# A sigmoid attention and token-mixing MLP kernel: a new hand-written order of its steps, loads, casts and PSUM banks

## Chip, core and metric

The kernel runs on one core of one Trainium2 chip. The metric is the device time of one execution in microseconds (us). The core has TensorE (PE in the profile; PEld are its weight loads), VectorE (DVE), ScalarE (ACT), GpSimd (POOL), and SyncE (SP), which issues most DMAs.

## The reference

Eight batches, twelve heads, 448 positions, head size 64. First attention with a sigmoid in place of a softmax, then a token-mixing MLP on its output:

```python
def _attn_ref(q, k, v):                       # q, k, v: 8 x 12 x 448 x 64, float32
    scores = scale * np.matmul(q, k.transpose(0, 1, 3, 2)) - np.log(S)
    attn = 1.0 / (1.0 + np.exp(-scores))
    return np.matmul(attn, v)

def _moe_ref(x, w_q, w_k, w_out):             # x: 8 x 448 x 768
    wq = x @ w_q                              # w_q, w_k: 768 x 64
    wk = x @ w_k
    W_tok = scale * np.einsum('bsd,btd->bst', wq, wk)
    mixed = np.einsum('bst,btd->bsd', W_tok, x)
    return np.maximum(mixed, 0.0) @ w_out     # w_out: 768 x 768
```

## The kernel before

**Tiling.** Heads are taken in groups of four, called quads; a batch has three, so there are 24, numbered 0 to 23. The positions of a quad are cut into 7 pieces of 64. For each piece `scores` (L319) runs four matmuls of 64 x 64 x 448 on the four quadrants of the PE array into a pair of PSUM banks, and ACT takes the sigmoid of the pair into one of 16 `at` buffers (L324): 168 such steps. `values` (L341) multiplies `at` by v and gathers the 7 pieces of a quad in another pair of banks; an eviction (L348, L350) puts the result into `xt`, transposed, and `tr_x` turns it to `xn` on PE with one eviction (L363 with 128 x 128 matmuls, or L379 with four times as many small ones; L368, L392).

**MLP.** When the three quads of a batch are there, `mlp_wqk` makes wq and wk (L416 with whole matmuls, L404 tiled into quadrants; the tiled form adds two halves with one more eviction, L411, L412), `mlp_wkn` transposes wk (L431, L437), `mlp_tmp` multiplies it by x (L445 whole, L460 tiled; L449, L464, L465), and `mlp_mix` makes the mixed rows (L484, L498), with scale and ReLU in the eviction (L469 on ACT, L471 on DVE). Pairs of batches then go through w_out in output blocks: `out_pair` (L530, evicted by L541 or L543) for batches 2 to 5, `out_halves` (L571; L576, L577) and `out_chunk` (L612; L645, L634) for the rest. Results go to one of three `o` buffers and from there to DRAM by DMAs that SP issues (L552, L585, L622), a few at the end by ACT.

**q and k.** They are loaded in float32 (L173, L179), into one of eight `ld` buffers that v's loads share, and cast to bfloat16 on POOL or DVE (L192, L215; v's casts are L209). Then their transposes: for most quads POOL swaps 32-partition blocks (L161, L164, L167) and DVE transposes 32 x 32 blocks (L276); for seven quads DVE does all (L269, L245); for a few PE transposes (L229, L237) and DVE evicts (L293, L307). The cast tiles of q and k have two buffers, those of v four.

**The order.** Nothing is scheduled at run time or by the compiler: each engine runs its instructions in the order in which the program issues them, and four tables set that order. `PLAN` is a string with a letter for each step: S a score piece, P (R, p) a piece of values, q, c, e, r and their partners the transposes, x and X the turn to `xn`, W (L, l, w) a step of wq and wk, N, U and T, M, O (Q, o, I, i) the MLP's steps, 1 a cast by DVE; variants of a letter choose the engine of an eviction or the tiled form. `BANKS` names the banks each step takes, in the same order. `ORDER` lists loads and casts; a dot ahead of an item says that DVE casts it when PLAN has a 1, all others are cast by POOL as soon as `ready` allows (buffers, and the cast of the quad before). `pump_loads` issues loads through SP in the order of `ORDER`, as long as the load eight places before has been cast in program order. From the load number `LATE` on it also stops after two loads until an output block is finished:

```python
            late = len(ring) > LATE
            if late and not allowed[0]:
                break
```

A load on SP waits for the cast that frees its buffer; what stands behind it on SP waits as well.

Of the kernel before, what the change touches and what calls it, by code (L numbers as in the profile page):

```python
# [17 lines left out]
def kernel(  # L18
# [29 lines left out]
    def pool(name, bufs, **kw):  # L48
# [16 lines left out]
    banks16 = banks.rearrange("p b x -> p (b x)").bitcast(BF16).rearrange("p (b x) -> p b x", b=8)  # L65

    BANKS = (
# [11 lines left out]
    )  # L79
    BANKS = BANKS.split()[::-1]  # L80

# [43 lines left out]
    def xt(u, j):  # L125
# [4 lines left out]


    PLAN = (
        "FFSSSFFKSSF1S1abSSSSSPrPsPSPSzPqSkSSP1PSPSxPSrPSSPSPsPPPPPPP"
        "SPPSSzWWWSWWWSxSSrXSNPsPPPPSPSPUSzSPPPSRMSPPPSqkSSXMSSMSRPPC"
        "SP1xSPPPcSSWWWxSWdWSWSQSrNsSSOOOSPPPSPPSPzPISISISISPPPPPSPSc"
        "PodoSSxUSPPMSPRPSPPScWQWSdMSWWoWWSMPPSPPrPSPPSNQosSSzSQOQxSO"
        "SXSSQcOdSCTSRPCrSPPPSCPPPPPSPPSPPCSOsWQSzSSWWoOSxWWWSPPMSPPP"
        "PRCSSScXXoodXSMNSQocSMPPSPPPSPPSUSdQSMQSoMocdSPPPPPPSPSWWXWS"
        "MSWWWXSSoNOSTSOcSOSrOQSQdSOSPPPPGRPSPsSPPRPPSPPSzoQSOSXSORPP"
        "SPScPPPoS1oSxQSOSLLLSdLLRLPSPPPPSPSoomcoQSNoGdSQxSQQST11PRSP"  # L140
        "RSPPRSooQcGOdcSSQOSQSOoSOSMoQGPPRSRPxPSPdQSQSOcSxQLLLSpLLSLP"
        "PpSPPPdSoSoxSo1SOSQOSOSNOStpRSRPSPPPRpSPpRypyplloGlGlllMQQyN"
        "QiTiiimIIGIMioOQOOQOQOQOQQoooOOOQ"
    )
    KIND = ["a"] + [t for t in PLAN if t in "qacer"]

# [546 lines left out]
    for t in wqks:  # L693
# [1 line left out]


    ORDER = (
# [4 lines left out]
    )  # L702
    BY = {"s": [], "v": []}
    for x in ORDER.split():
# [7 lines left out]
    done = dict.fromkeys("SPqkKxWNUMOCgz", 0)  # L712
    used, loaded, cast = set(), set(), set()

    LATE = 33
    ring = [("q", 0), ("k", 0)]

    allowed = [2]
# [1 line left out]
    def pump_loads():  # L720
        while len(loaded) < len(ORDER):

            late = len(ring) > LATE
            if late and not allowed[0]:
# [196 lines left out]
```

## Time and profile before

| | us |
|---|---|
| median of 3 runs (lowest, highest) | 183.65 (183.09, 185.05) |
| the profiled execution, its own time | 182.08 |
| its span in the profile | 180.3 |
| busy: PE, ACT, DVE, POOL | 168.8, 161.0, 144.7, 117.4 |
| HBM read, written | 35.78 MB, 11.01 MB |

The profile is of one execution. Busy time of PE is modelled: matmuls are pipelined and four quadrant matmuls run at once, so the mean time of one (357 ns for L319) is longer than the spacing of their starts. Times in the stretches below count from the start of the span. The granted TensorE clock is at 0.9 or more of full speed in all 40 slices of the page.

### The profile page before, as it was taken

How to read it: one execution, taken by the hardware profiler on the slowest of the kernel's cores; microseconds unless marked ns; L12 is line 12 of the kernel's file. 1: busy time of each engine (PE TensorE's matmuls, PEld its weight loads, DVE VectorE, ACT ScalarE, POOL GpSimd, SP SyncE). 2: the span in 40 equal slices, each digit the busy share in tenths (PEclk: the TensorE clock that was granted, in tenths of full speed). 3: DMA queues.
4: the chain of work that ended last, by engine and by line, in shares of the span. 5: the costliest groups of instructions: out<-in, count | busy, mean ns of one | idle time of the engine just before them, and what ended most of it. 6: DMA issues, size and time to landing. Idle time of an engine off the chain costs nothing.

```text
span 180.3 us, 7877 instructions
## 1 busy us (share of the span) xinstructions
PE 168.8 (94%) x3431; PEld 116.1 (64%) x3431; DVE 144.7 (80%) x230; ACT 161.0 (89%) x213; POOL 117.4 (65%) x160
## 2 busy tenths in 40 slices
PE   7867799989999999999999999999999999999990
PEld 7433456454476465656667788788888878787560
DVE  3667899999998899989989799987897976678401
ACT  4699999999999999999999999999999999966250
POOL 1074798992899999999999999999879410010000
PEclk9999999999999999999999999999999999999999
DMA  5999999998998899999999929779997432405686
GB/s 168 345 396 385 329 382 397 398 233 181 349 386 296 312 284 346 305 319 275 266 407 323 335 81 276 284 209 315 278 333 204 114 91 62 120 4 126 165 242 175
DMA packets 24787, 47.31 MB, mean 262 GB/s; under 512 B 3760, under 2 KB 18352, under 8 KB 24752
## 3 DMA queue, kind: packets, MB, share of 16 engines
q1 hardware_dynamic: 23472, 44.64, 76.3%
q0 software_dynamic: 800, 1.18, 3.6%
q10 hardware_dynamic: 480, 0.98, 1.7%
q8 instruction: 27, 0.44, 1.0%
q14 instruction: 8, 0.07, 0.1%
HBM read 35.78 MB, written 11.01 MB: 260 GB/s over the span
## 4 chain that ended last, share of the span: by engine, by line
PE 78%; DVE 13%; ACT 5%; issue 1%
PE banks L319 16%; PE banks L530 15%; PE banks L341 13%; PE banks L612 13%; ACT at L324 5%; PE banks L571 3%; PE banks L416 3%; DVE xt L350 3%; DVE qk L245 3%; PE banks L363 2%; PE banks L379 2%; PE banks L690 2%; PE banks L404 2%; PE banks L460 2%; DVE mx L471 2%; PE banks L484 1%
## 5 line engine op out<-in xcount | busy, mean ns | idle before, releaser
L324 ACT ACTIVATE at<-banks 128x896 bf16<-128x896 f32 x168 | 140.3, 940 | 2.0 <-PE banks L319 1.3
L319 PE MATMUL banks<-qk 64*64 64x448 bf16 x672 | 62.5, 357 | 5.1 <-ACT at L324 2.5
L341 PE MATMUL banks<-at,v 64*64 64x448 bf16 x672 | 45.7, 350 | 0.4 <-ACT at L324 0.4
L319 PEld LDWEIGHTS <-qk 64*64 64x64 bf16 x672 | 26.4, 105 | 24.2 <-issue 14.9
L530 PE MATMUL banks<-wout,mx 64*64 64x384 bf16 x672 | 36.1, 323 | 0.0
L192 POOL CAST qk<-k 128x896 bf16<-128x896 f32 x19 | 22.8, 1202 | 10.1 <-DMA k<-in_k_dram 9.7
L341 PEld LDWEIGHTS <-v 64*64 64x64 bf16 x672 | 23.7, 106 | 6.9 <-POOL v L209 0.8
L530 PEld LDWEIGHTS <-mx 64*64 64x64 bf16 x672 | 23.9, 107 | 3.5 <-issue 0.5
L192 POOL CAST qk<-q 128x896 bf16<-128x896 f32 x18 | 21.6, 1197 | 4.4 <-DVE qk L276 4.0
L350 DVE CAST xt<-banks 128x896 bf16<-128x896 f32 x21 | 22.6, 1081 | 2.2 <-PE banks L341 2.0
L612 PE MATMUL banks<-wout,mx 128*128 128x384 bf16 (+1 forms) x138 | 24.1, 320 | 0.0
L471 DVE TENSOR_SCALAR mx<-banks 128x1024 bf16<-128x1024 f32 (+3 forms) x23 | 21.2, 933 | 2.9 <-PE banks L484 1.9
L209 POOL CAST v<-v 128x896 bf16<-128x896 f32 x21 | 19.4, 933 | 1.6 <-DMA v<-in_v_dram 1.3
L612 PEld LDWEIGHTS <-mx 128*128 128x128 bf16 x138 | 12.5, 98 | 9.6 <-issue 2.5
L245 DVE STREAM_TRANSPOSE qk<-qk 32x448 f32<-32x448 f32 x28 | 17.8, 636 | 0.8
L161 POOL COPY swap<-qk 32x448 uint32<-32x448 uint32 x26 | 14.7, 565 | 2.8 <-DVE qk L192 1.3
L276 DVE STREAM_TRANSPOSE qk<-qk 128x448 f32<-128x448 f32 x26 | 16.1, 629 | 0.1
L164 POOL COPY qk<-qk 32x448 uint32<-32x448 uint32 x26 | 14.4, 554 | 1.5
L167 POOL COPY qk<-swap 32x448 uint32<-32x448 uint32 x26 | 14.4, 552 | 1.5
L413 POOL COPY wq<-wqk 64x448 bf16<-64x448 bf16 x3 | 1.7, 554 | 17.7 <-DVE wqk L412 17.7
L645 ACT COPY o<-banks 128x384 f32<-128x384 f32 x13 | 6.3, 483 | 5.7 <-PE banks L612 4.9
L392 DVE COPY xn<-banks 128x1024 bf16<-128x1024 bf16 (+1 forms) x15 | 9.5, 632 | 1.6 <-PE banks L379 1.4
(88 smaller groups left out, 203.3 us busy)
## 6 DMA issues: line engine op xcount, KB each, us to landing
q<-in_q_dram SPq DMA_DIRECT2D x24, 448.0 KB, 6.8
v<-in_v_dram SPq DMA_DIRECT2D x24, 448.0 KB, 6.7
k<-in_k_dram SPq DMA_DIRECT2D x23, 448.0 KB, 6.3
out_dram<-o SPq DMA_DIRECT2D x50, 192.0 KB, 4.1
wout<-in_moe_w_out_dram POOLq DMA_DIRECT2D x2, 576.0 KB, 9.1
wout<-wout SPq DMA_DIRECT2D x4, 288.0 KB, 9.8
out_dram<-o ACTq DMA_DIRECT2D x4, 192.0 KB, 3.5
k<-in_k_dram SPq DMA_DIRECT2D x1, 256.0 KB, 4.5
```

The source lines that it names most:

```text
L161: eng.tensor_copy(out=z[lo], in_=w[hi, 0])
L192: COPY[e](out=f[:, :, "qk".index(nm)].rearrange("p e i d y -> p e y i d"), in_=ld.pop((nm, n)).rearrange("p (y i e d) -> p e y i d", y=2, ...
L209: COPY[e](out=t16.rearrange("p b i d -> p (b i d)"), in_=ld.pop((nm, n)).rearrange("p b x -> p (b x)"),)
L245: nc.vector.transpose(out=qk[n][other : other + 32, h].rearrange("p t i n -> p (t i n)").bitcast(F32), in_=w[own : own + 32, 1 - h],)
L276: nc.vector.transpose(out=qk[n][:, t].rearrange("p t i n -> p (t i n)").bitcast(F32), in_=w)
L319: nc.tensor.matmul(sc[HALF[h], g, 0:S], qk[n][HALF[g], h, 1, i, :], qk[n][HALF[g], h, 0].rearrange("p i n -> p (i n)"), start=True, stop=True,
L324: inst = nc.scalar.activation(at, sc[:, :, 0:S], ACTF.Sigmoid, bias=attn_bias, scale=attn_scale)
L341: nc.tensor.matmul(ps[HALF[g], h, 0:S], ld["v16", n][HALF[h], g, i, :], ats[n, i][HALF[h], g, :], start=(i == 0), stop=(i == NI - 1),)
L350: read(fb, COPY[eng](out=xt(u, j)[:, :, 0:S], in_=ps[:, :, 0:S]))
L471: inst = nc.vector.tensor_scalar(dst, ps, moe_scale, 0.0, ALU.mult, ALU.max)
L530: nc.tensor.matmul(ps[HALF[x], y, 0:NB], mx[HALF[y], u, b, 64 * (i - 3 * y) : 64 * (i - 3 * y) + 64], wout16[HALF[y], b // 2, swapped(y, b ...
L612: nc.tensor.matmul(ps, mxs[w][:, 2 * S * c + m * P : 2 * S * c + (m + 1) * P], wout16[:, c, 0, w0:w1], start=(c == 0), stop=(c == NC - 1),)
```

## The change

`PLAN`, `BANKS`, `ORDER` and `LATE` are replaced; the code that reads them is not. The number of casts that DVE makes at a 1 in PLAN goes from eight (q1, k1, q4, k8, v19, v20, q22, v23) to nine (q1, k1, k2, q2, v8, q13, v15, v22, v23). The limit `LATE` goes from 33 to 69 of 73 loads. In PLAN the numbers of most letters stay; two batches' `mlp_tmp` change from the tiled to the whole form (T to U), one batch's `mlp_wqk` from tiled to whole with the second copy on ACT (L to w), two quads' `tr_x` from small to whole transposes (x to X), and some evictions change between DVE and ACT. PE has 3353 matmuls in place of 3431. The first and last lines of each table and the two small edits:

```diff
     BANKS = (
-        "01 23 45 7 7 67 01 23 5 5 45 67 01 4 45 23 67 01 23 45 67 01 23 45 67 23 45 23 67 45 23 "
+        "01 23 45 7 7 67 01 23 5 5 45 67 01 4 45 23 67 01 67 45 23 01 67 45 23 01 45 23 67 45 23 "
...
     PLAN = (
-        "FFSSSFFKSSF1S1abSSSSSPrPsPSPSzPqSkSSP1PSPSxPSrPSSPSPsPPPPPPP"
+        "FFSSSFFKSSF11SSab1SSSSSRSP1SPrPPsRzPRPSPPSPPqSPkSXSxSrSPPSR"
...
-        "QiTiiimIIGIMioOQOOQOQOQOQQoooOOOQ"
+        "ONIiItiiiimiGMOoQOoQoOQoQOoOoQQooo"
...
     ORDER = (
-        ".q1 .k1 k2 q2 v0 q3 k3 .q4 v1 k4 v2 w0 q5 k5 v3 q6 v4 k6 .k8 k7 w1 v5 w4 q7 q8 q9 v6 k9 "
+        ".q1 .k1 .k2 .q2 v0 v1 q3 k3 k4 q4 v2 w0 v3 k5 q5 q6 v4 k6 w1 k7 w4 v5 q7 q8 k8 q9 v6 k9 "
...
-    LATE = 33
+    LATE = 69
```

Two places where instructions move. The first is on DVE at the start, from the casts of quad 1 on. A number behind a name tells tiles apart: before, qk_260 holds the cast q and k of quad 2 and qk_357 those of quad 4; xt_111 to xt_113 are the first three quads' attention outputs. Before:

```order
L215 CAST q_247<-q_181 128x2x7x64
L215 CAST k_256<-k_183 128x2x7x64
L293 COPY qk<-banks 128x7x2x64 x2
L269 STREAM_TRANSPOSE qk<-qk_260 128x448 x2
L245 STREAM_TRANSPOSE qk<-qk_260 32x448 x4
L307 COPY qk<-banks 128x2x2x448
L192 CAST qk_357<-q_195 128x2x2x224
L350 CAST xt_111<-banks 128x2x448
L392 COPY xn<-banks 128x2x4x128
L269 STREAM_TRANSPOSE qk<-qk_357 128x448 x2
```

On the same engine and from the same place now; qk_286 holds quad 2 and qk_372 quad 4:

```order
L215 CAST q_251<-q_181 128x2x7x64
L215 CAST k_255<-k_183 128x2x7x64
L293 COPY qk<-banks 128x7x2x64 x2
L192 CAST qk_286<-k_185 128x2x2x224
L192 CAST qk_286<-q_187 128x2x2x224
L269 STREAM_TRANSPOSE qk<-qk_286 128x448 x2
L245 STREAM_TRANSPOSE qk<-qk_286 32x448 x4
L350 CAST xt_111<-banks 128x2x448
L350 CAST xt_112<-banks 128x2x448
L307 COPY qk<-banks 128x2x2x448
L368 COPY xn<-banks 128x4x256
L392 COPY xn<-banks 128x2x4x128
```

Both casts of quad 2 have come from POOL to DVE, ahead of quad 2's transposes; the cast of q4 has gone to POOL; and two evictions to xt stand ahead of L307, quad 3's last step, where one stood behind it.

The second place is on SP, where the first output blocks of `out_pair` are stored (L552). Loads are L173 and L179; the number is that of the `ld` tile. Before:

```order
L179 DMA v_2124<-in_v_dram 128x2x448
L173 DMA q_2126<-in_q_dram 128x896
L552 DMA out_dram<-o 64x2x384 x2
L179 DMA v_2294<-in_v_dram 128x2x448
L173 DMA k_2296<-in_k_dram 128x896
L552 DMA out_dram<-o 64x2x384 x2
L173 DMA k_2504<-in_k_dram 128x896
L173 DMA q_2506<-in_q_dram 128x896
L552 DMA out_dram<-o 64x2x384 x2
```

And now, from the same first store on:

```order
L552 DMA out_dram<-o 64x2x384 x2
L173 DMA k_2352<-in_k_dram 128x896
L179 DMA v_2354<-in_v_dram 128x2x448
L173 DMA q_2358<-in_q_dram 128x896
L173 DMA k_2362<-in_k_dram 128x896
L179 DMA v_2365<-in_v_dram 128x2x448
L173 DMA k_2369<-in_k_dram 128x896
L179 DMA v_2452<-in_v_dram 128x2x448
L173 DMA k_2456<-in_k_dram 128x896
L173 DMA q_2466<-in_q_dram 128x896
L552 DMA out_dram<-o 64x2x384 x4
```

Two loads stood between two blocks' stores; now nine do, and two blocks' stores follow each other behind them.

More of the change, by code (lines that the diff above doesn't have):

```diff
@@ L132 @@
     PLAN = (
-        "FFSSSFFKSSF1S1abSSSSSPrPsPSPSzPqSkSSP1PSPSxPSrPSSPSPsPPPPPPP"
[L134 to L142, printed above, removed]
-        "QiTiiimIIGIMioOQOOQOQOQOQQoooOOOQ"
+        "FFSSSFFKSSF11SSab1SSSSSRSP1SPrPPsRzPRPSPPSPPqSPSkSXSxSrSPPSR"
+        "sSPPPPSWWWSSWWzWxSNSrSUPPSPPSPPsPSPPPSPPCzSMSPPSSMqSkSXCSMPS"
+        "PRPSRxSPPSQScxSdWrWSSWWWWSsSOOSNOSRPPSPPPzPSiSISIcISPPSPdPPP"
+        "SPSQQS1xSUSPPMScPPPPSPSWdWQWSSMWWWoMCSPRSPRrPRSSPOQCNSsSSQzO"
+        "OSxOSXCcSSQOdSTSRP1PSPPRSPRPSPPPrSPSPooCsWWSSSWzWWWOQxSPRSPc"
+        "MPSRPRNXSSSdXXoOSMSOOSMPPSPPPScPPSUQSdSMQQSQPcSPRPGPPPSSXd1W"
+        "WSSWWWWXSQSNQcSdGOOSQSorSUSQSOpSRRRSRPsSPRpPSPPPPSQSOSQSRzpO"
+        "cSPRRPSPOSQSQdGQSSwXXwwwwwXSRNRoGpcSOSpdPpPSQSOS1oOSMQSoUcdS"
+        "pRSoRPSpPPSoSoGOSocSQSQOSoSQSxQGQGSPPpRpRSpo1OdSQSOLLSLLLcSL"
+        "PRPSPPpdSPOSoxSOxOSQSQSONQPSxRSPPpPSPtRPSpllPypPRlMlOmlMloxo"
+        "ONIiItiiiimiGMOoQOoQoOQoQOoOoQQooo"
     )
```

26 rows, old and new, of tables (BANKS, ORDER) are left out of this document.

## The prediction, made before the changed kernel had run

> **What bounds the kernel now.** First the page's busy times, then the span cut into stretches (columns: stretch, its length, and for PE, PEld, DVE, ACT and POOL the busy time with the number of instructions; then granted clock, DMA share, GB/s).
>
> ```profile
> PE 168.8 (94%) x3431; PEld 116.1 (64%) x3431; DVE 144.7 (80%) x230; ACT 161.0 (89%) x213; POOL 117.4 (65%) x160
> ...
> 20.00:60.00 40.00, 37.62 (x766) 21.77 (x766) 37.41 (x55) 39.73 (x50) 32.65 (x44) 1.00 1.00 328
> 60.00:101.60 41.60, 41.59 (x694) 25.64 (x687) 39.08 (x57) 41.05 (x53) 39.36 (x53) 1.00 0.98 318
> 101.60:155.60 54.00, 54.00 (x1378) 44.44 (x1374) 44.09 (x67) 52.93 (x70) 37.23 (x52) 1.00 0.68 207
> 155.60:176.20 20.60, 20.51 (x396) 14.72 (x388) 11.75 (x25) 11.54 (x24) 0.55 (x1) 1.00 0.52 133
> 176.20:180.30 4.10, 0.00 (x0) 0.00 (x0) 0.31 (x1) 0.00 (x0) 0.00 (x0) 0.95 0.56 169
> ```
>
> ACT is full to 155.6 us, PE reads as full from 60 us, and POOL and DVE lack 2.2 and 2.5 us of being full from 60 to 101.6. The cut at 101.6 is the 112th score (of 168): the score line alone has 444 matmuls in the window ahead of it, and 4 ran before 6.7 us, so 448, or 112 scores of 4.
>
> ```profile
> 6.70:101.60 94.90, 39.88 (x444) 16.64 (x436) 1.00 1.00 330
> ```
>
> Next the ACT rows: the timeline's first, then the ACT groups of 6.7 to 101.6 us (count, then busy time and mean), then those of 101.6 to 156.45 us.
>
> ```profile
> 6.74 18.82 ACT L324 ACTIVATE at<-banks 128x896 bf16<-128x896 f32 x23 [0.69 <-PE banks L319]
> ...
> L324 ACT ACTIVATE at<-banks 128x896 bf16<-128x896 f32 x110 | 91.1, 949 | 1.2 <-PE banks L319 0.9
> L645 ACT COPY o<-banks 128x384 f32<-128x384 f32 x6 | 2.9, 487 | 0.0
> L543 ACT COPY o<-banks 128x768 f32<-128x768 f32 x1 | 0.8, 800 | 0.2 <-PE banks L530 0.2
> L348 ACT CAST xt<-banks 128x448 bf16<-128x448 f32 x1 | 0.5, 532 | 0.1
> ...
> L469 ACT ACTIVATE mx<-banks 128x512 bf16<-128x512 f32 (+1 forms) x5 | 3.4, 689 | 0.1
> L541 ACT COPY o<-banks 128x384 f32<-128x384 f32 x4 | 2.0, 494 | 0.2 <-ACT at L324 0.2
> ```
>
> Unhindered sigmoids start every (18.82 - 0.94) / 22 = 0.81 us, so one overlaps the next by 0.13. From 6.7 to 101.6: 110 x 0.81 = 89.4, eight other ACT instructions 4.2, less their overlap of about 1.0; of 94.9 us some 2 are stalls. This stretch is bound by ACT.
>
> Last the PE groups from 101.6 to 176.2 us, whose busy times overlap, and from the chain of waits the time that a block takes when PE is not held up (start, time, count).
>
> ```profile
> L530 PE MATMUL banks<-wout,mx 64*64 64x384 bf16 x624 | 33.4, 323 | 0.0
> L319 PE MATMUL banks<-qk 64*64 64x448 bf16 x232 | 22.5, 351 | 0.0
> L341 PE MATMUL banks<-at,v 64*64 64x448 bf16 x252 | 17.3, 350 | 0.0
> L612 PE MATMUL banks<-wout,mx 128*128 128x384 bf16 (+1 forms) x66 | 10.0, 311 | 0.0
> L404 PE MATMUL banks<-xt,wqk 64*64 64x448 bf16 x72 | 5.1, 349 | 0.0
> L379 PE MATMUL banks<-ident,xt 64*64 64x64 bf16 x256 | 3.6, 193 | 0.0
> L460 PE MATMUL banks<-xn,wkn 64*64 64x384 bf16 x56 | 3.3, 323 | 0.0
> ```
>
> ```profile
> 50.74 0.38 PE banks L341 x8
> 63.62 0.38 PE banks L416 x2
> 69.90 0.38 PE banks L379 x32
> 87.81 0.45 PE banks L363 x8
> 92.60 0.77 PE banks L445 x8
> 95.38 0.49 PE banks L530 x12
> 128.58 0.59 PE banks L460 x14
> 166.20 9.93 PE banks L612 x66
> ```
>
> L530 costs 0.0408 us a matmul: 624 make 25.5, and the 96 of L571, same shape, 3.9. At 0.0475 (L341's 0.38 / 8) the 232, 252 and 72 of L319, L341 and L404 make 26.4. L612 adds 9.9, L379 3.0, L460 2.4: 71.1. Another 112 small matmuls cost at most 5.3 by L341's price. So of 74.6 us no more than 3.5 can be idle: from the 112th score PE's own work sets the time, and the last 4.1 us are the final eviction and store. The program's time is ACT's way to the 112th score, plus PE's work from there, plus 4.1.
>
> **The change part by part.** The sum is made on the profiled run, 182.08 us: the span of 180.3 and 1.78 around it. The median of the runs shown, 183.65, is 1.57 above that; I add the sum to the median.
>
> *PE's work after the 112th score.* By the two programs: 12 fewer L530 (-0.49), 24 fewer L404 (-1.14), 28 fewer L460 (-1.18), 64 fewer L379 (-0.76); 16 more L445 (+1.54), 6 more L416 (+1.14), 16 more L363 (+0.90), 8 more of 256 columns (at most +0.38). Sum +0.4, on the path. Bounds: 0, if the small prices are high, and +1.1, if ACT makes PE wait in the first 14 of the 56 scores (there the work is 11.3 us at these prices, below the 11.4 of 14 sigmoids and one more ACT instruction beside them, which makes 12.0). I take +0.4.
>
> *ACT to the 112th score.* Now five L645 copies, one half L348, one L541, one half L469, against six L645, one L543, one L348: five of 0.487 + 0.532 + 0.494 + 0.60 = 4.06, against 4.25. So -0.2. After it the others grow from 6.4 us (3.4 and 2.0, and two single ones of half a tile, about 0.5 each like L348's) to about 7.8: six halves of L469 at 0.60 (four halves are the 3.4 less about 1.0 for the whole one), three L541, one L543, and three single ones, a whole xt of about 0.95 (a sigmoid's size) and two halves. With 56 x 0.81 = 45.5 and less overlap of 1.5 that makes 51.8, under PE's 54.0: hidden. If the 2.2 us of cover went, it would cost up to 1.4.
>
> *The start: two casts come from POOL to DVE.* The rows that price it:
>
> ```profile
> 10.09 1.15 DVE L293 COPY qk<-banks 128x896 bf16<-128x896 bf16 x2 [0.70 <-PE banks L237]
> 11.06 1.19 POOL L192 CAST qk<-q 128x896 bf16<-128x896 f32 x1
> 13.49 2.64 DVE L245 STREAM_TRANSPOSE qk<-qk 32x448 f32<-32x448 f32 x4
> 17.43 0.38 PE L319 MATMUL banks<-qk 64*64 64x448 bf16 x4 [0.21 <-ACT at L324]
> 40.89 1.37 DVE L192 CAST qk<-k 128x896 bf16<-128x896 f32 x1
> 117.74 0.67 DVE L209 CAST v<-v 128x896 bf16<-128x896 f32 x1
> ```
>
> POOL's cast of q2 ends at 12.25 and the transposes of quad 2 end at 16.13 (13.49 + 2.64), so they take 3.88. The first score of quad 2 starts at 17.43, held by ACT: 1.3 us of slack. Now DVE casts both behind its copies, from 11.24, at 0.67 (the quickest such row) to 1.37 (the slowest): done 12.6 to 14.0, transposes 16.5 to 17.9. Against 17.43 that is 0.9 early to 0.5 late; +0.1. POOL is free of two casts there, which is worth nothing: it waits for loads.
>
> *The other casts.* Before, k8 (1.37) and q4 were DVE's in 20:60; now they are POOL's, and v8 comes instead. DVE, at 37.41 of 40, gains about a us of lead; v15, v22 and q13 replace v19, v20 and q22, later and at the same price. From -2 (all of ACT's stalls go) to +2 (they double); I take 0, as each quad's operands were ready only shortly ahead in the early rows above and the new order packs DVE as tightly.
>
> *The loads.* The limit on loads beyond the 33rd goes to the 69th, so they run up to nine in a row ahead of a store on SP. A gain is excluded while buffers, not the limit, hold them; I take 0 and price the harm below.
>
> Banks and the order of blocks within a packet: a shift of what waits on which bank; no row prices it but the 2 us of ACT stalls and PE's 3.5, which bound it from -2 to +2. Taken as 0.
>
> Sum: +0.4 - 0.2 + 0.1 = +0.3, so 182.4 by the profiled run, and 184.0 on the median.
>
> **The rivals.** *1. Stalls go (chance 0.2).* DVE is ahead after 45 us, POOL has one cast less while it is 39.36 of 41.60 busy, so quads come earlier: ACT's 2 us of stalls and about 1 of PE's 3.5 vanish: 184.0 - 3.0 = 181.0, at least -2.2 (181.8) to count. Against: ACT's stalls name PE (0.9 of its 1.2), whose order is as dense as before.
>
> *2. Stores stuck behind loads (0.17), slower.* Rows:
>
> ```profile
> L209 POOL CAST v<-v 128x896 bf16<-128x896 f32 x21 | 19.4, 933 | 1.6 <-DMA v<-in_v_dram 1.3
> ...
> out_dram<-o SPq DMA_DIRECT2D x50, 192.0 KB, 4.1
> ...
> SPq L173 <- POOL v L209: 12.7, 7, 4.2
> ...
> L161 POOL COPY swap<-qk 32x448 uint32<-32x448 uint32 x26 | 14.7, 565 | 2.8 <-DVE qk L192 1.3
> ...
> 117.38 1.45 POOL L161 COPY swap<-qk 32x448 uint32<-32x448 uint32 x2
> ```
>
> A load on SP waits until POOL has cast its buffer's last tenant (12.7 us in 7 waits already), and whatever stands behind it waits too. For the nine loads ahead of one store POOL has some 12 us to do: four casts of q or k (1.2 each), three of v (0.93), three pairs of swap copies (1.1 to 1.45), one small copy. An output buffer is reused three blocks later; 624 / 48 = 13 blocks in 74.6 us less the 20.6 of the end make one in 4.5, so 13.5 us, less 4.1 for landing: a store may be 9.4 late. Beyond that the copy to o waits, and with it PE's bank: 12 - 9.4 = 2.6 us in one place, at three such runs of loads 8: 186.6 to 191. Against: the loads go out while POOL leads, not all with 12 us to wait.
>
> *3. DVE too late early (0.12).* The two casts at 1.37 and two xt casts now ahead of L307 push quads 2 to 4 late, 0.5 to 0.8 each: 184.5 to 186.4, half of it over 1%. POOL may slow such casts and be slowed: its swap pair took 1.45 while DVE's 0.67 cast of 117.74 ran, against 2 x 0.565 on average, 0.3 more. Nine such casts against eight cost POOL 0.3 more by this row, on an engine that does one cast less, so nothing in the sum. [...]
>
> *4. The raised limit does nothing*, as buffers hold the loads anyway: then rival 2 is void and the forecast stands.
>
> **How the numbers follow.** Forecast 184.0, chance 0.51, itself from 182.7 to 185.4 (bounds of the PE term, the start's half us, and some of the runs' scatter, 183.09 to 185.05). 1% of 183.65 is 1.84, about what a measurement of this kernel tells from no change: below 181.8 is faster, above 185.5 slower. Faster 0.2 (rival 1). Slower: rival 2, half of rival 3, and 0.02 of the forecast's edge: 0.25. The rest, 0.55, is the same. For 8 in 10: from 181.2, leaving out 0.08 of rival 1, to 186.8, leaving out 0.12 of rivals 2 and 3.
>
> **What would show it.** In the changed profile: the 112th score at 101.3 to 102.3 us; PE's work from there to its end 74.7 to 75.4; sigmoids of quad 2 without a gap near 17.9; SP stores issued within 9 us of their copy. The prediction is wrong if PE has idle time by name after 102 us (rival 2 if it goes back to o and a store, else a bank), or if the 112th score comes before 100.

## The result, and the profile after

| | before | after |
|---|---|---|
| median of 18 runs each, beside each other (us) | 182.25 | 183.26 |
| ratio, with its 95% interval | 1 | 1.0068 [1.0046, 1.0091] |
| profiled execution, its own time and span (us) | 182.08, 180.3 | 185.1, 183.3 |
| the same two kernels timed again (29 and 12 runs, us) | 182.37 | 183.44 |
| ratio then | 1 | 1.0044 [1.0023, 1.0066] |

The change costs 0.8 to 1.2 us by these ratios, less than 1%. That is inside the range of the prediction, whose sum was +0.3. Its 184.0 us stood on the three runs shown, whose median was 183.65; over more runs the kernel before takes 182.25, so the forecast's time is 0.7 high and its difference 0.5 to 0.9 low; that the two errors partly cancel is luck. The ratios, here and below, are taken over the fast runs alone and are not quotients of the medians (1.0055 here). The first profile of the changed kernel is of one of its longest executions: 185.1 us, 1.8 above its own median. Read against the profile of before it gives 3.0 us to explain, most of which is scatter. So the changed kernel was profiled once more, with an execution of 183.32 us (span 181.5), and this second profile is the one read here.

First the busy times on the page of the first profile, which hardly differ from before (PE 168.8, DVE 144.7, ACT 161.0, POOL 117.4). No engine's total shows a loss of 3 us; what counts is where in the run the work lies, and who waits there.

```profile
PE 169.4 (92%) x3353; PEld 115.2 (63%) x3353; DVE 143.4 (78%) x229; ACT 160.2 (87%) x213; POOL 118.2 (64%) x158
```

Then both kernels cut at the same places of their work: where the last matmul of the 14th score starts, of the 98th, 112th, 126th, 140th, 154th and 168th, and at the end of PE. Columns: stretch, its length, and for PE, PEld, DVE, ACT and POOL the busy time and the number of instructions; then granted clock, DMA share, GB/s. Before:

```profile
16.63:88.75 72.12, 68.66 (x1280) 40.13 (x1279) 67.17 (x98) 71.62 (x91) 61.84 (x81) 1.00 1.00 317
88.75:101.58 12.83, 12.83 (x244) 8.47 (x235) 11.96 (x16) 12.52 (x16) 11.99 (x18) 1.00 0.99 355
101.58:113.95 12.37, 12.37 (x290) 10.20 (x282) 10.99 (x18) 12.26 (x17) 11.69 (x16) 1.00 0.72 224
113.95:128.24 14.29, 14.29 (x386) 11.85 (x388) 12.03 (x18) 13.79 (x18) 13.22 (x19) 1.00 0.81 261
128.24:142.51 14.27, 14.27 (x369) 11.97 (x363) 11.92 (x19) 13.81 (x20) 11.79 (x18) 1.00 0.83 255
142.51:155.20 12.69, 12.69 (x346) 10.13 (x342) 8.77 (x15) 12.69 (x17) 0.55 (x1) 1.00 0.30 74
155.20:176.20 21.00, 20.91 (x404) 15.04 (x396) 12.15 (x25) 11.94 (x24) 0.55 (x1) 1.00 0.53 134
```

And the second profile of the changed kernel:

```profile
16.06:88.84 72.78, 70.04 (x1318) 41.07 (x1319) 68.02 (x102) 71.94 (x92) 63.30 (x81) 1.00 1.01 332
88.84:101.87 13.03, 13.03 (x244) 8.08 (x236) 12.47 (x18) 12.62 (x17) 12.19 (x17) 1.00 0.84 282
101.87:113.49 11.62, 11.62 (x263) 8.41 (x260) 9.82 (x16) 11.62 (x16) 11.07 (x15) 1.00 0.94 322
113.49:128.75 15.26, 14.88 (x324) 11.96 (x319) 12.25 (x19) 14.01 (x20) 13.33 (x17) 1.00 0.82 271
128.75:143.31 14.56, 14.56 (x365) 11.42 (x360) 10.36 (x15) 14.56 (x21) 13.42 (x21) 1.00 0.54 134
143.31:156.63 13.32, 13.32 (x390) 11.04 (x382) 8.87 (x13) 12.82 (x17) 0.59 (x2) 1.00 0.41 94
156.63:177.40 20.77, 20.68 (x370) 15.25 (x367) 12.48 (x25) 10.79 (x22) 0.56 (x1) 1.00 0.53 131
```

The 112th score comes at 101.87 against 101.58. From there to PE's last matmul it takes 75.44 us against 74.53 (101.58 to 176.11, 101.87 to 177.31). So nearly all of the loss lies behind the 112th score, and the largest single step is 113.49:128.75, with 0.97 us more than before and, of the five up to the 168th score, the only one in which PE is not full (14.88 of 15.26).

One thing makes this table sharp. From the 70th to the 168th score, the profiles of kernels that have the same order agree in each stretch within 0.02 us, but for single stops of PE that are told below, though their whole times differ by two us: the first profile has 11.62, 15.26, 14.55, 13.32 too. What scatters is the first 65 us.

### The profile page after: what moved, and what is told of

Its sections match the earlier page's. It is cut to its first block, busy times and chain, and to the rows that moved or that the text cites. A ratio compares the mean times of both kernels' runs of the same rounds, so it can differ in the third digit from the quotient of the medians.

```text
span 183.3 us, 7718 instructions
## 1 busy us (share of the span) xinstructions
PE 169.4 (92%) x3353; PEld 115.2 (63%) x3353; DVE 143.4 (78%) x229; ACT 160.2 (87%) x213; POOL 118.2 (64%) x158
## 4 chain that ended last, share of the span: by engine, by line
PE 76%; ACT 7%; DVE 7%; DMA 6%; POOL 1%; issue 1%; POOLq 0%; ACTq 0%
PE banks L530 15%; PE banks L319 15%; PE banks L341 14%; PE banks L612 12%; ACT at L324 6%; DMA v<-in_v_dram 4%; PE banks L416 3%; PE banks L571 3%; PE banks L363 2%; DMA q<-in_q_dram 2%; PE banks L379 2%; DVE xt L350 2%; PE banks L445 2%; PE banks L484 2%; PE banks L498 2%; PE banks L404 1%
## 5 line engine op out<-in xcount | busy, mean ns | idle before, releaser
L319 PE MATMUL banks<-qk 64*64 64x448 bf16 x672 | 60.6, 356 | 3.7 <-ACT at L324 1.5
L341 PE MATMUL banks<-at,v 64*64 64x448 bf16 x672 | 46.3, 350 | 1.6 <-ACT at L324 0.9
L530 PE MATMUL banks<-wout,mx 64*64 64x384 bf16 x672 | 37.2, 323 | 0.0
L209 POOL CAST v<-v 128x896 bf16<-128x896 f32 x20 | 18.9, 952 | 14.7 <-DMA v<-in_v_dram 14.2
L530 PEld LDWEIGHTS <-mx 64*64 64x64 bf16 x672 | 23.4, 107 | 3.9 <-issue 0.3
L471 DVE TENSOR_SCALAR mx<-banks 128x512 bf16<-128x512 f32 (+3 forms) x24 | 20.9, 879 | 3.4 <-PE banks L498 1.9
L161 POOL COPY swap<-qk 32x448 uint32<-32x448 uint32 x26 | 15.2, 583 | 1.6
L413 POOL COPY wq<-wqk 64x448 bf16<-64x448 bf16 x2 | 1.1, 554 | 18.2 <-DVE wqk L412 18.2
L543 DVE COPY o<-banks 128x768 f32<-128x768 f32 x9 | 8.6, 954 | 4.8 <-ACT at L324 3.8
L392 DVE COPY xn<-banks 128x1024 bf16<-128x1024 bf16 (+1 forms) x13 | 8.4, 647 | 3.4 <-PE banks L379 3.4
```

The source lines that it names most:

```text
L161: eng.tensor_copy(out=z[lo], in_=w[hi, 0])
L209: COPY[e](out=t16.rearrange("p b i d -> p (b i d)"), in_=ld.pop((nm, n)).rearrange("p b x -> p (b x)"),)
L319: nc.tensor.matmul(sc[HALF[h], g, 0:S], qk[n][HALF[g], h, 1, i, :], qk[n][HALF[g], h, 0].rearrange("p i n -> p (i n)"), start=True, stop=True,
L341: nc.tensor.matmul(ps[HALF[g], h, 0:S], ld["v16", n][HALF[h], g, i, :], ats[n, i][HALF[h], g, :], start=(i == 0), stop=(i == NI - 1),)
L471: inst = nc.vector.tensor_scalar(dst, ps, moe_scale, 0.0, ALU.mult, ALU.max)
L530: nc.tensor.matmul(ps[HALF[x], y, 0:NB], mx[HALF[y], u, b, 64 * (i - 3 * y) : 64 * (i - 3 * y) + 64], wout16[HALF[y], b // 2, swapped(y, b ...
```

## The experiments

Twelve runs followed. They were taken at three times, so each was timed beside the kernel before; the last column is its ratio to that, with the 95% interval.

| run | edit | median us | ratio to before |
|---|---|---|---|
| after_again | the changed kernel | 183.44 | 1.0044 [1.0023, 1.0066] |
| e1_slots | other load buffers | 183.73 | 1.0056 [1.0032, 1.0081] |
| e4_w_on_pool | wq's copy from ACT to POOL | 183.11 | 1.0014 [0.9986, 1.0042] |
| e2_late40 | LATE 69 to 40 | 192.37 | 1.0531 [1.0489, 1.0573] |
| e3_before_late69 | before, LATE 33 to 69 | 184.73 | 1.0148 [1.0100, 1.0197] |
| e6_fill | idle matmuls at 13 to 16 us | 183.25 | 1.0063 [1.0037, 1.0089] |
| e8_start_on_pool | k2, q2 cast on POOL | 183.16 | 1.0052 [1.0026, 1.0078] |
| e9_tiled | as e4, and two tmp steps tiled | 183.27 | 1.0065 [1.0040, 1.0091] |
| e11_half_tmp | as e4, half of two tmp steps | 184.06 | one execution, no ratio |
| e12_combo | e4, e6 and e8 together | 182.74 | 1.0038 [1.0020, 1.0056] |
| e13_w_late60 | as e4, LATE 60 | 182.88 | 1.0033 [1.0012, 1.0054] |
| e14_before_late40 | before, LATE 33 to 40 | 182.13 | 1.0006 [0.9989, 1.0023] |

**The changed kernel again.**

> The changed kernel once more, as the measure for the runs beside it, and for a second profile, since the first one (185.1 us) lies 1.8 us above its own median of 183.3. Every theory expects 183.3 us, a ratio of 1.005 to 1.009 to before. What the theories differ on is where the loss lies in the second profile. First theory (a late start): the 42nd score starts at least 1.0 us later than before's 39.70 us, most of that lost between the 28th and the 42nd. Rival (the end): the 112th score comes no more than 0.5 us later than before's 101.58 us and the loss follows it. If both stretches lose less than in the first profile (2.0 us to the 112th score, 1.0 us from there), what shrinks was scatter of that one execution.

The first theory, a late start, came from the first profile alone (42nd score at 41.12 us) and falls here: 40.02 against 39.70. The rival holds, with the loss behind the 112th score.

**The load buffers.** In the changed kernel the loads of k4 and q4 take the buffers of v0 and v1, whose casts on POOL come late.

```diff
-    p_ld = pool("ld", 8)
+    p_ld = pool("ld", 1)
+    SLOTS = list("0123456701236071425360714253607142536710425367102534671025364710253647102")[::-1]
...
-            t = p_ld.tile([P, 2 * NI * HD], F32, tag="ld", name=nm + "32")
+            t = p_ld.tile([P, 2 * NI * HD], F32, tag="ld" + SLOTS.pop(), name=nm + "32")
```

> The changed kernel with its eight load buffers handed on in another order: the load of k4 follows the DVE cast of q1 in its buffer and no longer the GpSimd cast of v0, that of q4 follows the cast of k1 and no longer that of v1, and v2 and v3 take the buffers of v0 and v1. Order of instructions, engines of the casts and banks are as in the changed kernel. First theory (the two loads that wait for casts of v0 and v1 hold up every load behind them on SP, so GpSimd and then the MLP of batch 0 come late): k4's load goes out near 11 us instead of 14.27, GpSimd's waits for loads between 20 and 33 us mostly go, the 42nd score comes 0.7 us or more earlier than in the changed kernel, and the time is 0.6 to 1.4 us below it, a ratio to before of 0.999 to 1.004. Rival (the loss is in the order and the banks, or at the end): the loads come earlier and the time stays within 0.3 us of the changed kernel's, a ratio of 1.005 to 1.009.

The rival held: the loads go out earlier and the time stays. The timeline shows SP's issues and POOL's casts (start, time, what, and the wait before it). The changed kernel (second profile):

```profile
13.53 0.34 SPq L173 DMA_DIRECT2D k<-in_k_dram  x1
14.85 0.34 SPq L173 DMA_DIRECT2D q<-in_q_dram  x1
...
12.56 0.94 POOL L209 CAST v<-v 128x896 bf16<-128x896 f32 x1 [11.26 <-DMA v<-in_v_dram]
```

With other buffers (its lines are numbered one higher):

```profile
9.77 0.34 SPq L174 DMA_DIRECT2D k<-in_k_dram  x1
10.91 0.34 SPq L174 DMA_DIRECT2D q<-in_q_dram  x1
...
13.82 0.93 POOL L210 CAST v<-v 128x896 bf16<-128x896 f32 x1 [12.52 <-DMA v<-in_v_dram]
```

The two loads go out 3.8 and 3.9 us earlier, but they hardly land earlier: k4 at 18.39 us in place of 17.48, q4 at 19.54 in place of 19.88. The loads land one behind another, 1.1 to 1.2 us apart in this run, and the row is late from its third load on (7.64 in place of 5.95), which landed before either of the two was issued; v0, late by 1.26 us, stands in that row. So the delay is hardly the edit's: in the other profiles of the changed kernel and its variants the third load lands anywhere between 5.60 and 7.16. The stretch from 9 to 13.5 us in both, the second one with other buffers, has the DMA engines full (share 1.04):

```profile
9.00:13.50 4.50, 2.95 (x43) 1.68 (x40) 3.22 (x6) 4.50 (x7) 0.94 (x1) 1.00 1.04 396
```

```profile
9.00:13.50 4.50, 3.44 (x47) 1.71 (x48) 3.67 (x8) 4.00 (x5) 0.00 (x0) 1.00 1.04 399
```

**The second copy of wq.** The change lets ACT make this copy (L423) for one batch, where POOL made it from DVE's result.

```diff
-        "cSPRRPSPOSQSQdGQSSwXXwwwwwXSRNRoGpcSOSpdPpPSQSOS1oOSMQSoUcdS"
+        "cSPRRPSPOSQSQdGQSSWXXWWWWWXSRNRoGpcSOSpdPpPSQSOS1oOSMQSoUcdS"
```

> The changed kernel with the second copy of wq of the last batch back on GpSimd, as the other batches have it; the changed kernel has six blocks whose copy is ScalarE's. Theory of the end (the copy on ScalarE waits 0.87 us for VectorE and the next sigmoids and PE behind it): 0.4 to 0.9 us below the changed kernel, a ratio to before of 1.002 to 1.005. Theory of the late start: that wait lies in a stretch which PE bounds, so no more than 0.2 us, a ratio of 1.005 to 1.008. If GpSimd is behind there, its copies come later than ScalarE's did and the time is 0.3 to 1 us above the changed kernel.

The theory of the end holds, by the trace; the ratio of 1.0014 lies just below its 1.002 to 1.005. The second profile of the changed kernel, ACT, DVE and PE:

```profile
121.86 0.52 ACT L423 CAST wq<-banks 64x448 bf16<-64x448 f32 x1 [0.87 <-DVE wqk L421]
...
121.14 0.62 DVE L421 CAST wqk<-banks 128x448 bf16<-128x448 f32 x1
...
121.48 0.38 PE L319 MATMUL banks<-qk 64*64 64x448 bf16 x4
...
122.43 0.22 PE L431 MATMUL banks<-ident,wqk 64*64 64x64 bf16 x3 [0.38 <-ACT wq L423]
```

ACT's copy is put down to DVE's copy ahead of it and PE's next step to ACT's. By the table of banks (`4 5 0 5 01 67 4`) the step L431 writes bank 4, the very bank that both copies read: PE can't go on until the later one is done. With the copy on POOL, which reads DVE's result and not the bank, L431 follows its score by 0.41 us in place of 0.95, and the stretch takes 14.74 in place of 15.26:

```profile
122.04 0.38 PE L319 MATMUL banks<-qk 64*64 64x448 bf16 x4
...
122.45 0.19 PE L431 MATMUL banks<-ident,wqk 64*64 64x64 bf16 x2
...
114.04:128.78 14.74, 14.74 (x325) 11.88 (x320) 12.17 (x19) 13.53 (x19) 13.86 (x18) 1.00 0.84 285
```

All other stretches behind the 70th score are as they were, so 0.52 us is the price of this copy. The medians bear it out, though none of them alone: the five timings of kernels that differ from this one only ahead of it have ratios of 1.0068, 1.0044, 1.0056, 1.0063 and 1.0052, mean 1.0057; the three with the copy on POOL and no other edit that shows behind the 112th score (e4, e12, e13) 1.0014, 1.0038 and 1.0033, mean 1.0028. The difference is 0.0029 of 182.2, or 0.53 us.

**The limit on loads, from both sides.**

```diff
-    LATE = 69
+    LATE = 40
```

> The changed kernel with the limit on loads put back from the 69th towards the 33rd: to the 40th (36 and 33 can't be had with this order, since a cast of it would come ahead of its load). Theory that the loads ahead of the stores cost time (loads in a row on SP that wait for a buffer, stores and the output buffers behind them): 0.5 us or more below the changed kernel, a ratio to before of 1.000 to 1.004. Theory of the late start, and that buffers hold the loads anyway: within 0.3 us of the changed kernel, a ratio of 1.005 to 1.009. If the later limit was needed, casts in the middle wait for loads and the time is 0.5 us or more above the changed kernel.

```diff
-    LATE = 33
+    LATE = 69
```

> The kernel before with one number changed, the limit on loads from the 33rd to the 69th. The changed kernel with the limit at the 40th took 192.37 us, 9 us more than with the 69th, so its order needs late loads to run ahead. Theory that the limit alone is worth nothing where buffers hold the loads (the prediction's fourth rival): a ratio to before of 0.998 to 1.002. Theory that loads in a row ahead of stores cost time on SP (its second rival): 1.005 or more, with stores that go out later than before and copies to the output buffers that wait for a DMA. If the limit held loads back in before as well: 0.997 or less.

Both went against the prediction, which took the limit for idle. With 40 the changed order starves. The waits of that kernel (engine, what it waited for, us in total, times, longest):

```profile
POOL qk L192 <- DMA k<-in_k_dram: 12.1, 2, 9.9
POOL v L209 <- DMA v<-in_v_dram: 11.8, 2, 11.1
...
DVE v L209 <- DMA v<-in_v_dram: 8.2, 1, 8.2
```

DVE's cast of v waits 8.2 us for its load, and everything behind it on DVE as well: the 140th to the 154th score takes 23.84 us in place of 14.55. So the new order and the new limit are one edit: the order needs loads ahead of stores.

In the kernel before, the same limit costs 2.7 us (184.73 - 182.08), and not by late stores: no engine waits for a store longer than before. Its PE stops inside a block of twelve equal matmuls:

```profile
132.10 0.68 PE L530 MATMUL banks<-wout,mx 64*64 64x384 bf16 x10
133.83 1.32 PE L530 MATMUL banks<-wout,mx 64*64 64x384 bf16 x26 [1.05 <-issue]
```

"Issue" is a wait for nothing that the profile names. Among the DMA packets of each profile are 26 or 27 of 16 KB that it marks as instructions (here `q8 instruction: 27, 0.44, 0.9%`: count, MB, share of the engines). Here these packets start at 118.0, 125.6 and 131.5 us, in the kernel before at 117.3, 122.7, 127.6 and 132.7; PE goes on 1.5 us after the one of 131.5 has ended. Ten such stops stand in the profiles, each 1.3 to 1.5 us behind the end of such a packet, with 0.4 to 1.4 us between two starts of PE: two here (127.3 us, which the profile puts down to ACT, and 132.5), one in e14 (0.47), one in e11 (0.78), one early in e6, and one each near 60 us in both profiles of the changed kernel, e6, e9 and e13. A count ties them to the packets. Ahead of the ten stops PE has loaded weights 352, 992 (five times), 2016, 2272, 2400 and 2528 times, each 96 more than a multiple of 128; and 128 matmuls with their weight loads are 256 instructions. The first profile of the changed kernel has 6712 instructions of PE recorded and 26 such packets, 258 to a packet. From these counts and times the author infers that the packets carry PE's instructions and that PE waits for them at these places; no run shows that by itself. Two more stops (e9, 0.45, and one here at 95.5 us, 0.47) stand at no such place.

The three stretches of 14 scores that hold the three stops of this profile are 0.49, 0.36 and 1.36 us longer than in the kernel before, 2.21 of the 2.64 us between the two spans. That the loads hold these packets back was not tried by itself: it stays open.

With the copy on POOL, a limit between the two:

```diff
-    LATE = 69
+    LATE = 60
```

> The changed kernel with the second copy of wq on GpSimd and the limit on loads at the 60th in place of the 69th. At the 40th the casts waited up to 11 us for their loads; in the kernel before, the 69th cost 2.7 us. Theory that a limit has a best place between, with stores that go out earlier and loads that still come in time: 0.3 us or more below the copy on GpSimd alone, a ratio to before below 0.999. Theory that every load held back comes late for a cast that the new order has packed tightly: 0.5 us or more above it, a ratio of 1.004 or more. If the last nine loads have slack: 1.000 to 1.003.

The last nine loads have slack: 1.0033, a little above the 1.003 written down, and each stretch behind the 70th score as in the run with the copy on POOL. The limit decides somewhere between 40 and 60.

And in the kernel before:

```diff
-    LATE = 33
+    LATE = 40
```

> The kernel before with the limit on loads at the 40th in place of the 33rd; at the 69th it took 2.7 us more. Theory that each load that goes out ahead of a store costs time in that order, the earlier ones as well: a ratio to before of 1.002 to 1.006. Theory that only long rows of loads ahead of a store cost: 0.998 to 1.002. If the 33rd holds loads back that are wanted: 0.997 or less, and then this kernel beats both.

Level with before (1.0006); its 128th to 143rd us hold the stop of 0.47 us named above.

**The start.** The change puts the casts of k2 and q2 on DVE. Undone:

```diff
-        "FFSSSFFKSSF11SSab1SSSSSRSP1SPrPPsRzPRPSPPSPPqSPSkSXSxSrSPPSR"
+        "FFSSSFFKSSF11SSabSSSSSRSPSPrPPsRzPRPSPPSPPqSPSkSXSxSrSPPSR"
...
-        ".q1 .k1 .k2 .q2 v0 v1 q3 k3 k4 q4 v2 w0 v3 k5 q5 q6 v4 k6 w1 k7 w4 v5 q7 q8 k8 q9 v6 k9 "
+        ".q1 .k1 k2 q2 v0 v1 q3 k3 k4 q4 v2 w0 v3 k5 q5 q6 v4 k6 w1 k7 w4 v5 q7 q8 k8 q9 v6 k9 "
```

> The changed kernel with the casts of k2 and q2 at the start back on GpSimd, all else as changed. The prediction put their move to VectorE at +0.1 us, between 0.9 early and 0.5 late. If that holds: within 0.5 us of the changed kernel, a ratio to before of 1.002 to 1.009. Rival: GpSimd has its casts of v0 and v1 and of q3 and k3 behind those two, so with them back it is late for the values of the first quads, and the time is 0.5 to 2 us above the changed kernel, which would say that the move was a gain of the changed kernel. If the move costs time, as the two loads that come later through it, 0.5 us or more below.

1.0052, level with the changed kernel: the move is worth nothing within some 0.6 us (the two intervals together). What DVE's casts cost there depends on which of DVE and POOL starts first. In the second profile of the changed kernel POOL cast v0 from 12.56 to 13.50, 0.05 us ahead of DVE's cast of q2:

```profile
12.04 0.67 DVE L192 CAST qk<-k 128x896 bf16<-128x896 f32 x1
12.61 1.42 DVE L192 CAST qk<-q 128x896 bf16<-128x896 f32 x1
```

In the run with other load buffers POOL was idle until 13.82, and the same cast of q2 took half:

```profile
12.70 0.66 DVE L193 CAST qk<-q 128x896 bf16<-128x896 f32 x1
```

In the first profile of the changed kernel DVE began 0.05 us ahead of POOL, and POOL's cast of v0 is the one that took longer, 1.39 in place of 0.94:

```profile
12.80 0.66 DVE L192 CAST qk<-q 128x896 bf16<-128x896 f32 x1
...
12.85 1.39 POOL L209 CAST v<-v 128x896 bf16<-128x896 f32 x1 [11.55 <-DMA v<-in_v_dram]
```

**A clock that halves.** Three of the first five profiles of the changed kernel and its variants show a granted clock of 0.50 for some 3 us from 15 to 16 us on (e1, e2 and e4; 0.50 from 17 to 18 us in each). The stretches 13 to 16 and 16 to 20 us, of the second profile and of e4:

```profile
13.00:16.00 3.00, 1.53 (x20) 0.47 (x16) 2.90 (x5) 3.00 (x5) 2.49 (x3) 1.00 0.99 323
16.00:20.00 4.00, 3.86 (x92) 2.44 (x92) 2.98 (x5) 4.00 (x7) 2.19 (x3) 1.00 0.91 287
```

```profile
13.00:16.00 3.00, 1.50 (x20) 0.71 (x23) 2.87 (x6) 3.00 (x5) 2.69 (x4) 1.00 0.84 283
16.00:20.00 4.00, 4.00 (x53) 2.69 (x49) 1.99 (x3) 3.09 (x4) 2.09 (x2) 0.57 0.91 276
```

The same 28 matmuls take 1.52 us in the one and 2.69 in the other. The edit that puts PE to work there, with two matmuls of zeros for each V:

```diff
-        "FFSSSFFKSSF11SSab1SSSSSRSP1SPrPPsRzPRPSPPSPPqSPSkSXSxSrSPPSR"
+        "FFSSSFFKSSF11SSab1SSSVSVSRVSP1VSPrPPsRzPRPSPPSPPqSPSkSXSxSrSPPSR"
...
+        if t == "V":
+            for b in map(int, BANKS[-1]):
+                take(b)
+                nc.tensor.matmul(banks[:, b], zeros[:, 0:P], zeros, start=True, stop=True)
+            continue
```

> The changed kernel with ten idle matmuls of zeros (512 columns, two ahead of five of the scores 11 to 15), written to the banks that the score behind them overwrites. In three of the five profiles of the changed kernel and its variants the granted clock of TensorE goes to 0.50 for some 3 us from about 15.5 us on, behind a stretch from 13 us on in which TensorE is 0.28 to 0.57 busy; where it does, the 28th score comes 0.7 to 1.3 us later behind the 14th. Theory that the sparse stretch brings the low clock: the profile shows 1.00 from 13 to 20 us, nearly all of the executions a mean clock above 0.994 (5 of 12 in the changed kernel, 20 of 29 in before), and the time falls by 0.2 to 0.4 us, a ratio to before of 1.002 to 1.004. Theory that the low clock comes from elsewhere: the share of executions below 0.994 stays, and the time stays or grows by what the matmuls hold up scores, up to 0.4 us.

```profile
13.00:16.00 3.00, 2.59 (x26) 0.81 (x22) 2.87 (x6) 3.00 (x5) 2.19 (x3) 1.00 0.95 326
16.00:20.00 4.00, 3.77 (x97) 2.33 (x100) 1.89 (x3) 3.68 (x6) 2.97 (x3) 1.00 0.94 267
```

Right on the cause; the price stays open. With PE 2.59 of 3 us busy, none of 24 executions (this kernel and e12) has a mean clock below 0.994; 7 of 12 of the changed kernel have, and of the kernels without these matmuls that ran beside the two 6 of 12 (e8), 5 of 12 (e9) and 6 of 11 (e13). The median doesn't fall (1.0063). But that isn't the low clock's price: e4's profile, with the low clock, is 1.34 us behind this one at the 28th score (29.32 against 27.98) and 0.26 at the 70th (64.88 against 64.62), with no edit between, and 0.71 of the lead goes in the 14 scores up to the 70th (13.36 us in place of 12.65), where PE stops as in e3 with nothing named, behind its 992nd weight load:

```profile
59.18 0.74 PE L341 MATMUL banks<-at,v 64*64 64x448 bf16 x12
60.50 0.38 PE L341 MATMUL banks<-at,v 64*64 64x448 bf16 x4 [0.58 <-issue]
```

e12, which has the idle matmuls and no such stop, is 0.34 us ahead of e8, which lacks them and has the low clock, at the 28th score (28.19 against 28.53) and still 0.35 at the 70th. And within e8 the six executions with the low mean clock average 183.32 us, the other six 182.89. So the low clock may cost some 0.4 us where it comes; the medians don't show it.

> The changed kernel with the three edits together that cost nothing or gained alone: the second copy of wq on GpSimd (0.5 us less behind the 112th score), the casts of k2 and q2 back on GpSimd (no difference in the median), the idle matmuls ahead of the scores 11 to 15 (no execution with the low clock, and no difference in the median). If only the copy counts: 0.3 to 0.5 us below the changed kernel, a ratio to before of 1.001 to 1.004. If the start's edits help each other: level with before, 0.997 to 1.001. The remaining 0.4 us of TensorE's work behind the 112th score stay in any case.

1.0038: the copy counts; the start's edits add nothing that the median shows.

**Is it PE's work behind the 112th score?** First the two steps from wkn to tmp there, in the form that costs PE less by the prediction's prices.

```diff
-        "WSSWWWWXSQSNQcSdGOOSQSorSUSQSOpSRRRSRPsSPRpPSPPPPSQSOSQSRzpO"
-        "cSPRRPSPOSQSQdGQSSwXXwwwwwXSRNRoGpcSOSpdPpPSQSOS1oOSMQSoUcdS"
+        "WSSWWWWXSQSNQcSdGOOSQSorSTSQSOpSRRRSRPsSPRpPSPPPPSQSOSQSRzpO"
+        "cSPRRPSPOSQSQdGQSSWXXWWWWWXSRNRoGpcSOSpdPpPSQSOS1oOSMQSoTcdS"
```

> The changed kernel with the second copy of wq of the last but two batches on GpSimd, as in the run before, and the two steps from wkn to tmp that come behind the 98th score in the form of four tiles (14 matmuls, two banks, and VectorE adds the halves) in place of the whole form (8 matmuls, one bank), as the kernel before has them. By the prices of the prediction the whole form costs 8 x 0.096 = 0.77 us and the tiled one 14 x 0.0406 = 0.57. Theory that TensorE's own work sets the time from the 112th score: of the 74.91 us from there to its last matmul that the copy on GpSimd alone left, 0.2 to 0.4 us go, so 74.5 to 74.7, and the ratio to before is 0.999 to 1.002. Rival: two more banks taken and one more VectorE step each make the scores behind them wait: 75.0 us or more.

The rival's number came true, 75.35 us from the 112th score to PE's end in place of 74.91, with 0.2 us of work less in each of two stretches. Its mechanism isn't shown. The first of the two takes 11.67 us in place of 11.62, the second, from the 140th to the 154th score, 14.96 in place of 14.55:

```profile
127.41:142.37 14.96, 14.83 (x370) 12.19 (x366) 10.88 (x16) 14.60 (x21) 13.26 (x21) 1.00 0.52 140
```

That second stretch holds the stop inside a block of L530 named above (0.45 us), which is all of its 0.41. What remains is that neither stretch got shorter. So work was taken away with no bank and no step added:

```diff
-        for m in range(4):
+        ms = range(2) if u in (4, 5) else range(4)
+        for m in ms:
...
-                    start=(m == 0), stop=(m == 3),
+                    start=(m == 0), stop=(m == ms[-1]),
```

> The changed kernel with the second copy of wq on GpSimd, and half of the matmuls left out (4 of 8) in the two steps from wkn to tmp near 106 and 130 us, so that tmp of two batches holds half of its sum; every wait and every step behind them stays. Theory that TensorE's own work sets the time from the 112th score: 4 x 0.096 = 0.38 us go in each of the two stretches, from the 112th score to the 126th 11.62 becomes 11.2 to 11.3, from the 140th to the 154th 14.55 becomes 14.1 to 14.2, and from the 112th score to the last matmul 74.91 becomes 74.1 to 74.2. Rival: the waits between the engines set it (the tiled form had 0.2 us less of work in each of these stretches and did not shorten either): no stretch shortens by more than 0.1.

```profile
102.45:114.06 11.61, 11.49 (x260) 8.60 (x256) 9.80 (x16) 11.61 (x16) 11.06 (x15) 1.00 0.92 310
...
129.61:144.11 14.50, 14.42 (x360) 11.63 (x355) 10.45 (x15) 14.50 (x21) 13.37 (x21) 1.00 0.55 131
```

Of 0.38 us taken from PE in each, the first stretch gives back 0.01 and the second 0.05. The theory falls for these two stretches. From the 112th score to the last matmul it takes 75.66 us, not the 74.1 to 74.2 of the theory, since the stretch between the two holds the stop of 0.78 us and takes 15.55 in place of 14.74. ACT's column would explain the two: 11.61 of 11.61 and 14.50 of 14.50. Where PE has less to do, ACT is already full. That ACT sets the time there is argued, not shown: no run gave it less to do in these stretches.

## Why the prediction came out right, and where its steps did not

**The two-part bound: half right.** The 112th score came at 101.87, inside the 101.3 to 102.3 that was written down; half a us of it is PE's stop near 60 us (the 14 scores up to the 70th take 13.15 us, and 12.65 in the profiles without it). From there "PE's own work sets the time" is too simple. Behind the 112th score PE and ACT are both full or nearly so, and a stretch takes about the longer of the two. By the prediction's prices (small matmuls by their columns, an estimate) PE's work in the four stretches of 14 scores is 12.01, 14.10, 14.24 and 12.66 us before and 11.28, 14.41, 14.44 and 13.53 now. Measured: 12.37, 14.29, 14.27 and 12.69 before; 11.62, 14.74, 14.55 and 13.32 with the copy on POOL. The second and the fourth, in which ACT has idle time now, follow PE's work; in the first and the third ACT has none, and there taking PE's work away gave nothing. In the third, ACT's instructions other than sigmoids went from 2.74 to 4.08 us and its idle time from 0.46 us to none, so that stretch's 0.28 us may be ACT's and not PE's.

**PE's work, +0.4:** without the copy on ACT, 74.91 against 74.53, so +0.38. The size agrees, in part by luck: in two of the four stretches PE's work is not what the time follows, as e11 shows.

**ACT, -0.2 to the 112th score, and more copies "hidden" behind it: the failing step.** The first part is small and right in sign (the 84th to the 98th score 0.25 shorter, the 98th to the 112th 0.20 longer). The second is what was mis-sized: the wq copy was counted as half a tile of ACT's time under 2.2 us of cover, at nothing. It costs 0.52, since the cover was counted over 54 us and the copy sits at one place where PE waits for the bank it reads. PE's wait, not ACT's busy time, is its price. With it the sum would have been +0.8, the lower end of what was measured.

**The start, +0.1:** within the error of its undoing. DVE's two casts took 0.67 and 0.66 to 1.42, close to the bounds written down (0.67 to 1.37); quad 2's sigmoids have no gap (18 of them end to end from 11.79 to 26.58 us in the second profile).

```profile
11.79 14.79 ACT L324 ACTIVATE at<-banks 128x896 bf16<-128x896 f32 x18
```

**The loads, 0, "while buffers, not the limit, hold them": wrong, without harm.** The limit does hold loads: put back to 40 it costs 8.9 us in this order (192.37 against 183.44), raised to 69 it costs 2.7 in the other. Behind the 112th score the stretches of the second profile leave no loss for the loads beside the copy and the 0.38, so the number came out and its reason did not: that is luck. The fourth rival falls with it.

**The other rivals.** Stalls did not go. Stores were not stuck: between 100 and 130 us the copies to o that end at 105.3, 115.7 and 119.4 are stored from 110.9, 122.6 and 124.6 on, within the 9 us named, and no copy waits for a store. DVE was not late at the start.

**DVE's casts beside POOL's copies.** The prediction put what a cast of DVE's costs POOL at 0.3 us, from one row of the kernel before, which gives two of POOL's copies in one figure (1.45). One by one that trace has 0.55 for the copy that starts ahead of DVE's cast and 0.84 for the one that starts during it, 0.29 more, with 0.43 us shared. The second profile has this meeting again, here with the copies one by one:

```profile
56.13 0.55 POOL L161 COPY swap<-qk 32x448 uint32<-32x448 uint32 x1
56.74 0.84 POOL L161 COPY swap<-qk 32x448 uint32<-32x448 uint32 x1
57.64 1.17 POOL L164 COPY qk<-qk 32x448 uint32<-32x448 uint32 x2
...
56.37 0.79 DVE L209 CAST v<-v 128x896 bf16<-128x896 f32 x1
```

POOL's first copy starts ahead of DVE's cast and takes no longer than its neighbours (0.55). DVE's cast takes 0.17 longer than the 0.62 of such a cast beside an idle POOL (at 149.02 us in the kernel before), and shares 0.31 us with that copy. POOL's second copy starts while DVE's cast runs, takes 0.29 longer, and shares 0.43 us with it. Each time the one that starts later takes longer by what the two share, less some 0.14 us. The casts at the start agree: 0.76 us of 0.89 lost by DVE where POOL is first, 0.45 of 0.60 by POOL where DVE is first. So the 0.3 us of the prediction's row is one copy that took no longer and one that did. Its conclusion stands: nothing of this shows in the sum.

Of the loss of about 1.0 us (0.0057 of 182.2) 0.5 is the copy, shown by its undoing, and 0.4 lies in the other stretches behind the 112th score, as much as PE's prices foretell, though whether PE or ACT sets each of them is not shown; what is left can't be told from the start's scatter. No kernel here beats the one before; e4 and e14 are level with it.

## What to carry to other kernels

An instruction that moves to an engine with time to spare isn't free if another engine waits for the buffer it reads (0.52 us here): price it by who needs that bank next, in its own stretch, not by the engine's idle share over a third of the run. Before explaining a difference of a few us between two profiles, take a second profile of the same kernel and cut both at the same places of the work: here single stretches repeat within 0.02 us where whole times scatter by 2. And a limit that has to be low in one order of work may have to be high in another (here the high one costs 2.7 us in the one, the low one 8.9 in the other), so test it in both.

## What the runs showed of the hardware

- PE's granted clock went to 0.50 for some 3 us behind a stretch in which PE was busy 1.50 of 3 us (e4), and the same 28 matmuls took 2.69 us in place of 1.52. Behind 1.53 of 3 us busy, in the second profile of the changed kernel, it stayed at 1.00; 7 of 12 executions of that kernel have a mean clock below 0.994. With the idle matmuls, PE 2.59 of 3 us busy (e6's profile), none of 24 has.
- PE can stop with nothing named to wait for, also inside a row of equal matmuls (1.05 us in a block of L530, e3). Ten stops (0.4 to 1.4 us between two starts) came 1.3 to 1.5 us behind the end of a 16 KB packet that the profile marks as instructions, and whole multiples of 128 weight loads apart (with their matmuls 256 instructions; PE's 6712 recorded ones over 26 packets make 258). There are 26 or 27 such packets in a profile and at most two such stops. Whether PE waited for what these packets carry, and why at these ones alone, stays open.
- With the DMA engines full (396 and 399 GB/s from 9 to 13.5 us), loads of 448 KB landed 1.1 to 1.2 us apart (e1_slots); issuing two of them 3.8 and 3.9 us earlier brought one in 0.34 us earlier and the other 0.91 later, in an execution whose loads were 1.2 us late already.
- Where a cast of DVE's and a cast or copy of POOL's ran at the same time, the one that started second took longer by the time that the two shared, less some 0.14 us (0.17 to 0.76 us in the five meetings told above).
